# A fused transformer block on one core: two weight slices loaded later, fewer warm-up matmuls, a clamp on another engine

## The chip, the core and the metric

The kernel runs on one core of one Trainium2 chip. The metric is the device time of one execution in microseconds (us); lower is better. The core has five engines that run their own instruction streams and wait for each other through semaphores: TensorE (PE in the profile; PEld is its weight load), VectorE (DVE), ScalarE (ACT), GpSimd (POOL) and SyncE (SP), which here only issues DMA transfers.

## The reference

Everything is bfloat16 outside of the accumulators. With S = 2048 tokens and width 448:

```python
phi = lambda t: jnp.where(t > 0, t + 1, jnp.exp(t)) + 1e-6
q, k, v = split(layernorm(x) @ wqkv)            # 16 heads of 28
pq, pk = phi(q), phi(k)
kv = einsum("bhsd,bhse->bhde", pk, v);  z = einsum("bhsd->bhd", pk)
num = einsum("bhqd,bhde->bhqe", pq, kv)
den = einsum("bhqd,bhd->bhq", pq, z)[..., None] + 1e-6
h = x + (num / den).reshape(B, S, D) @ wo
y = layernorm(h)
h2 = h + (gelu(y @ w_gate) * (y @ w_up)) @ w_down   # inner width 1792
```

So it is a linear attention, whose state `kv` and `z` sums over all tokens, followed by a gated MLP, each behind a layer norm and with a residual.

## The kernel before, in words

The 2048 tokens are 16 tiles of 128. Each piece of work is a named task, and the name says what it is and for which tile. `_Graph` derives the dependencies from the buffers that a task reads and writes, and `ORDERS` gives, engine by engine, the order in which the tasks are issued: five strings, written out in full, for TensorE, ScalarE, VectorE, GpSimd and SyncE. Nothing is decided at run time: an engine takes its tasks in that order and waits at each one for its semaphores. A task that waits therefore holds back everything behind it on its engine. Line numbers below are those of the kernel before. Most matmuls are issued by one helper, so they carry line 430 in the profile; the tile names tell them apart.

**Head.** SyncE and ScalarE issue the loads of x and of the K, V and Q weights. TensorE has nothing to work on yet and runs matmuls on a tile of ones, `warm1` (16, half of the rows each) and `warm0` (`WARM`, line 253, each 128 columns, line 454). For every tile of x VectorE makes the statistics (`bnst`, `bnag`, lines 462 and 463), ScalarE the reciprocal deviation (`ln`, `rstd`), and VectorE (tiles 0 to 3) or GpSimd (the others) the normalised tile (`norm`, lines 486 and 487). Tiles 0 to 3 are transposed on TensorE (`tr0` to `tr3`, line 495) and copied out by ScalarE (`ev`, line 523); the others go through transposing DMAs (`xT`, line 526) after ScalarE has written a copy of their last columns (`dup`, line 525).

**K, V and state.** For each tile `k` and `v` are the matmuls of K and V. Both use the two halves of TensorE's rows at once: in `k` the upper half works on the bank of K and the lower half on that of V, in `v` the other way round. A pass whose bank was last written by the other half waits until that work has drained. For phi(K), ScalarE takes the exponential (`ek`, line 565), GpSimd clamps it (`cl`, line 566), VectorE takes the maximum with K and adds (`ph`, line 568). ScalarE copies V out (`evv`, line 570). `acc..a` and `acc..b` add the tile to the state in two banks. The Q chunks (512 tokens, two passes `qa` and `qb`) are spread among the tiles; the first ones go through `eq` (ScalarE), `cq` (GpSimd, line 626) and `pq` (VectorE, line 627), the later ones through `eq` and `rq` (ScalarE, lines 616 and 617), `cq` and `pq` (VectorE, lines 618 and 619). When all 16 tiles are in, `kz1` and `kz2` (VectorE, lines 642 and 643) write the state with masks.

**Attention output.** For tiles 0 and 1, one at a time: `nd` (TensorE, line 672), `rd` and `om` (VectorE: reciprocal, product, lines 654 and 655), `tro` (transpose on TensorE, line 681), `evo` (ScalarE), `wo` (lines 688 and 689), `hr` (VectorE: residual, line 660), statistics, `normh`, `wrap` (a copy of 64 columns, line 695), `trh` (transpose on TensorE, line 702), `evh` (ScalarE line 707, VectorE line 709). The other tiles go in pairs: `nd..a`, `nd..b`, `rd`, `om`, a transposing DMA for each (`oT`, line 729), `wo..a`, `wo..b`, `hr`, statistics, `normh` on GpSimd, and a transposing DMA (`hT`, line 750).

**MLP.** Token chunks of 2, 2, 4, 4 and 4 tiles. For each chunk `gu` tasks multiply with the gate slice on the upper half of the rows and the up slice on the lower half, `ge` (ScalarE, line 830) is the gelu, `hm` (VectorE, line 832) the product with up, which frees the banks. Two pairs of banks alternate, so a `gu` waits for the `ge` and `hm` of the one two before it. Then come `down` and `out` (residual, line 756) and the store. A table load on ScalarE (`tbl2`, line 850) stands between the exponentials and the first gelu.

**SyncE's queue around the change.** After the twelve `xT`, SyncE issues the loads of `wo` (`dwo` and three more), then seven gate/up slices, a gate half `dwg` and an up half `dwu` for each, 224 KB apiece, then `oT2`, `oT3`, then the whole of `w_down` (`dwd`, 1568 KB), then the later transposes and the stores. Slice k is needed by the k-th pair of matmuls of a `gu` accumulation, so slices 5 and 6 come last in it.

Of the kernel before, what the change touches and what calls it, by code (L numbers as in the profile page):

```python
# [7 lines left out]
ALU = mybir.AluOpType  # L8
# [222 lines left out]
def bass_sequential_preLN__linear_attn_block__glu_gated_geglu__prompt_kernel(  # L231
    nc, A_x, A_wqkv, A_wo, B_x, B_w_gate, B_w_up, B_w_down, out, cfg=None
):
    cfg = dict(cfg or {})
# [678 lines left out]
```

## Time and profile before

| What | Value |
|---|---|
| Three runs, us | 196.69, 196.73, 196.25; median 196.69 |
| The profiled execution, us | 196.70 |
| Its span (first to last instruction), us | 194.9 |
| TensorE busy | 190.3 us, 98% of the span |
| VectorE busy | 116.3 us, 60% |
| ScalarE busy | 78.2 us, 40% |
| GpSimd busy | 42.0 us, 22% |
| Granted TensorE clock, mean over the span | 0.999 |
| Moved by DMA | 17.53 MB, mean 90 GB/s |

How to read it: a row of the timeline gives the start in us from the span's start, the duration, the engine, the line, the operation, output and inputs, the shape, and in brackets the idle time before it and what ended that. A matmul's duration in a row includes its way through the array, so successive ones overlap; the distance between starts is the cost in a sequence. The chain of waits is followed back from the last instruction; a step in it is work that nothing else could have hidden. The span leaves out 1.8 us of the execution's time.

### The profile page before, as it was taken

The numbers are of one execution on the slowest core, as the hardware profiler recorded it, in microseconds if no ns is written. First come the engines' busy times: TensorE is split into PE (matmuls) and PEld (weight loads), VectorE is DVE, ScalarE is ACT, GpSimd is POOL, SyncE is SP. The second block draws the span as 40 slices with busy tenths as digits, with TensorE's granted clock in tenths as the row PEclk, the third lists the DMA queues.
The fourth block names the chain that finished last, engine by engine and source line by source line (L and its number), as shares of the span: only waits on it lengthen the run. The fifth ranks groups of instructions, "written<-read, shape, count | busy, mean of one in ns | idle before, by whom it ended". The sixth has DMA issues, their size and how long they took to land.

```text
span 194.9 us, 5336 instructions
## 1 busy us (share of the span) xinstructions
PE 190.3 (98%) x2192; PEld 137.9 (71%) x2192; DVE 116.3 (60%) x301; ACT 78.2 (40%) x205; POOL 42.0 (22%) x90
## 2 busy tenths in 40 slices
PE   7999999999999999999999999999999999999994
PEld 7556658754588977976675577877778779899554
DVE  2989735368998946843967745756735443431512
ACT  3689866669784212220442441233232442411100
POOL 3099974300050310500500500500500000000000
PEclk9999999999999999999999999999999999999999
DMA  6944558999836052152062250172040000010111
GB/s 191 377 116 97 81 110 185 247 248 205 260 103 110 15 101 50 50 105 62 10 129 46 46 106 2 30 117 51 5 94 28 23 0 0 3 47 3 47 47 47
DMA packets 37256, 17.53 MB, mean 90 GB/s; under 512 B 28272, under 2 KB 36336, under 8 KB 37232
## 3 DMA queue, kind: packets, MB, share of 16 engines
q1 hardware_dynamic: 36352, 16.45, 36.8%
q10 hardware_dynamic: 880, 0.75, 1.2%
q8 instruction: 17, 0.28, 0.6%
q14 instruction: 7, 0.06, 0.1%
HBM read 8.72 MB, written 1.84 MB: 54 GB/s over the span
## 4 chain that ended last, share of the span: by engine, by line
PE 96%; issue 1%; ACT 1%; DVE 1%; POOL 0%; DVEq 0%; ACTq 0%; POOLq 0%
PE ps L430 87%; PE ps L780 6%; PE ps L454 2%; DVE x_sb L660 1%; PE ps L495 1%; ACT xn L617 1%; PE ps L681 0%; ACT xnT L523 0%; PE ps L672 0%; DVE x_sb L756 0%; POOL ones_bf L395 0%; POOL eps_t L398 0%; ACT pqT L616 0%; DVEq L196 0%; ACTq L196 0%
## 5 line engine op out<-in xcount | busy, mean ns | idle before, releaser
L430 PE MATMUL ps<-hnT,wgu_sb 64*128 64x512 bf16 (+1 forms) x980 | 90.4, 333 | 0.0
L430 PEld LDWEIGHTS ps<-hnT,wgu_sb 64*128 64x128 bf16 x980 | 64.5, 94 | 18.6 <-DVE hh L832 1.7
L830 ACT ACTIVATE gl<-ps 128x256 bf16<-128x256 f32 x112 | 36.9, 381 | 89.3 <-PE ps L430 88.2
L832 DVE TENSOR_TENSOR hh<-ps,gl 128x256 bf16<-128x256 f32 x112 | 42.5, 415 | 35.7 <-ACT gl L830 31.5
L430 PE MATMUL ps<-wd_sb,hh 64*128 64x448 bf16 x336 | 34.4, 349 | 0.0
L430 PEld LDWEIGHTS ps<-wd_sb,hh 64*128 64x128 bf16 x336 | 25.6, 94 | 6.2 <-DVE x_sb L756 0.2
L430 PE MATMUL ps<-wkv_sb,xnT 64*128 64x448 bf16 x192 | 22.4, 350 | 0.4 <-ACT xnT L523 0.4
L462 DVE BATCH_NORM_STATS2 st<-x_sb 128x6 f32<-128x448 bf16 x32 | 18.7, 611 | 2.6 <-DMA x_sb<-in_A_x_dram 2.6
L756 DVE TENSOR_TENSOR x_sb<-ps,x_sb 128x448 bf16<-128x448 f32 (+1 forms) x17 | 9.9, 591 | 16.6 <-PE ps L430 9.8
L474 POOL TENSOR_SCALAR ln<-mv 128x2 f32<-128x2 f32 x7 | 1.6, 223 | 75.0 <-DVE mv L463 74.9
L568 DVE SCALAR_TENSOR_TENSOR pk<-ps,tm 128x448 bf16<-128x448 f32 x16 | 9.8, 620 | 9.6 <-POOL tm L566 7.1
L430 PE MATMUL ps<-xnT,wq_sb 64*128 64x512 bf16 x112 | 14.9, 377 | 0.2 <-ACT xn L617 0.2
L430 PEld LDWEIGHTS ps<-wkv_sb,xnT 64*128 64x128 bf16 x192 | 10.1, 94 | 6.3 <-issue 0.8
L430 PE MATMUL ps<-wo_sb,oT 64*128 64x448 bf16 x98 | 12.1, 350 | 0.1
L660 DVE TENSOR_TENSOR x_sb<-ps,x_sb 128x448 bf16<-128x448 f32 x16 | 9.4, 618 | 4.6 <-PE ps L430 4.4
L780 PE MATMUL ps<-wd_sb,hh 128*128 128x448 bf16 (+1 forms) x70 | 10.8, 315 | 0.0
L566 POOL TENSOR_SCALAR tm<-e 128x448 bf16<-128x448 bf16 x16 | 8.9, 559 | 6.4 <-ACT e L565 5.5
L487 POOL TENSOR_SCALAR hn<-x_sb,nm,rs 128x448 bf16<-128x448 bf16 x14 | 10.0, 720 | 0.8 <-POOL rs L476 0.2
L565 ACT ACTIVATE e<-ps 128x448 bf16<-128x448 f32 x16 | 8.5, 541 | 3.5 <-PE ps L430 2.2
L780 PEld LDWEIGHTS ps<-wd_sb,hh 128*128 128x128 bf16 x70 | 6.7, 98 | 4.3 <-issue 0.4
L655 DVE TENSOR_TENSOR o_sb<-ps,rd 128x448 bf16<-128x448 f32 x16 | 9.4, 612 | 0.1
L570 ACT ACTIVATE v<-ps 128x448 bf16<-128x448 f32 x16 | 8.4, 542 | 2.1 <-PE ps L430 2.1
(69 smaller groups left out, 140.4 us busy)
## 6 DMA issues: line engine op xcount, KB each, us to landing
out_dram<-x_sb SPq DMA_DIRECT2D x15, 112.0 KB, 1.7
wgu_sb<-in_B_w_gate_dram SPq DMA_DIRECT2D x7, 224.0 KB, 6.1
wgu_sb<-in_B_w_up_dram SPq DMA_DIRECT2D x7, 224.0 KB, 6.4
wd_sb<-in_B_w_down_dram SPq DMA_DIRECT2D x1, 1568.0 KB, 8.3
x_sb<-in_A_x_dram SPq DMA_DIRECT2D x2, 448.0 KB, 5.3
wkv_sb<-in_A_wqkv_dram ACTq DMA_DIRECT2D x2, 336.0 KB, 3.7
x_sb<-in_A_x_dram SPq DMA_DIRECT2D x3, 224.0 KB, 4.2
wo_sb<-in_A_wo_dram SPq DMA_DIRECT2D x2, 336.0 KB, 4.4
```

The lines of the kernel that those rows point to most:

```text
L430: ins = e.matmul(o_, l_, r_, start=s_, stop=p_, **kw)
L462: op("dve", lambda e: e.bn_stats(st[:, t, :], src_ap), [b_src], [b_st[t]], "%sbnst%d" % ("" if mv is mv1 else "h", t), 0.53, key, after=after)
L487: return lambda e: e.tensor_scalar(dst, src[:, t, :], nm[:, t:t + 1], rs[:, t:t + 1], ALU.add, ALU.mult)
L565: act_exp(lambda e: e.activation(e1[:, ie, :], oK, AF.Exp), bank(bk), [b_e1[ie]], "ek%d" % t, _c_act(D), kk)
L566: op("pool", lambda e: e.tensor_scalar(tm1[:, ie, :], e1[:, ie, :], 1.0 + EPS, 0.0, ALU.min, ALU.max), [b_e1[ie]], [b_tm1[ie]], "cl%d" % t ...
L568: op("dve", lambda e: e.scalar_tensor_tensor(pk[:, i, :, 0:GW], psK3, EPS, tm1[:, ie, :].rearrange("p (g e) -> p g e", g=NG), ALU.max, ALU ...
L655: op("dve", lambda e: e.tensor_tensor(o_sb[:, so, oc:oc + D].rearrange("p (a e) -> p a e", e=28), nd3[:, :, 0:28], rd[:, i, :].unsqueeze(2 ...
L660: op("dve", lambda e: e.tensor_tensor(h_sb[:, u, :], ps[:, b, 0:D], x_sb[:, u, :], ALU.add), bank(b) + [b_x[u]], [b_h[u]], "hr%d" % u, 0.5 ...
L756: op("dve", lambda e: e.tensor_tensor(x_sb[:, t, c0:c1], ps[:, bk, c0:c1], h_sb[:, t, c0:c1], ALU.add), bank(bk) + [b_h[t]], [bo], "out%d% ...
L780: ins = e.matmul(ps[:, bk, c0:c1], hh[:, j, hsl(t)], wd_sb[:, j, c0:c1], start=(j == 0), stop=(j == NJ - 1))
L830: G.add("act", lambda e, gi=gi, cs_=cs_, psG=psG: e.activation(gl[:, gi, cs_], psG[:, cs_], AF.Gelu_apprx_tanh), r=bank(BK_G[i]), w=[b_glh ...
L832: op("dve", lambda e, dst=dst, srcU=srcU, srcL=srcL: e.tensor_tensor(dst, srcU, srcL, ALU.mult), bank(BK_U[i]) + [b_glh], [b_ar[j_][t % HR ...
```

## The change

Five things change together.

1. `WARM` goes from 38 to 33: five fewer matmuls in `warm0`.
2. SyncE issues gate/up slices 0 to 4 as before, then `oT2` and `oT3`, then slices 5 and 6, then `dwd`.
3. The clamps `cl14` and `cl15` are issued on VectorE and no longer on GpSimd.
4. `trh` waits for `wrap` only ahead of its last transpose, the one that reads the wrapped columns.
5. All five order strings are written anew.

What moves in the orders, as far as the prediction speaks of it: on TensorE `acc3a` moves ahead of `k6`, `acc4a` ahead of `k7`, `acc8b` and `acc9b` ahead of `k12` and `v11`; `acc13a` and `acc14a` move ahead of `qa20`, `acc14b` and `acc15b` ahead of `qb20`; `qb31` moves from between `wo2a` and `wo2b` to behind `trh0`; `wo14a`, `wo14b` and the later `down` passes are placed differently among the `gu` tasks. On ScalarE `ek15` moves ahead of `evv15`, `evh0` ahead of `eq14`, and `rq14` behind the gelus of the third `gu`. On VectorE the memset of `pk`'s padding (`pkones`) moves to the head; `pq8` moves up between `om1` and `rd2`; `om4` and `om5` both come before the first `hm`; `cq14` and `cq10` come behind it. On GpSimd some norms and clamps swap places, `negm12` moves ahead of `cq1`, and `powwarm` moves to the head.

```diff
-    WARM = 38
+    GU_AHEAD = 5
+    CL_DVE = cfg.get("cl_dve", (14, 15))
+    WARM = 33
...
-        for k in range(7):
-            prev = [dma(wgu_sb[0:64, k, :], wg3[:, k, :], [b_wg[k]], "dwg%d" % k, 64 * FF * 2, after=prev, key=20.0)]
-            prev = [dma(wgu_sb[64:128, k, :], wu3[:, k, :], [b_wu[k]], "dwu%d" % k, 64 * FF * 2, after=prev, key=20.0)]
+        def load_gu(ks, prev, key):
+            for k in ks:
+                prev = [dma(wgu_sb[0:64, k, :], wg3[:, k, :], [b_wg[k]], "dwg%d" % k, 64 * FF * 2, after=prev, key=key)]
+                prev = [dma(wgu_sb[64:128, k, :], wu3[:, k, :], [b_wu[k]], "dwu%d" % k, 64 * FF * 2, after=prev, key=key)]
+            return prev
+
+        prev = load_gu(range(GU_AHEAD), prev, 20.0)
...
-            op("pool", lambda e: e.tensor_scalar(tm1[:, ie, :], e1[:, ie, :], 1.0 + EPS, 0.0, ALU.min, ALU.max),
+            op("dve" if t in CL_DVE else "pool", lambda e: e.tensor_scalar(tm1[:, ie, :], e1[:, ie, :], 1.0 + EPS, 0.0, ALU.min, ALU.max),
...
-            def ftrh(e):
+            def ftrh(e, W):
                 ins = None
-                for k in (0, 1, 2, 4, 5, 6, 3):
+                for n, k in enumerate((0, 1, 2, 4, 5, 6, 3)):
+                    if n in (0, 6):
+                        W(n)
...
-            G.add("pe", ftrh, r=[b_hn[sh], b_hnd[sh], b_ident], w=bank(bh), name="trh%d" % t, dur=_c_mm(128, 7), key=ka)
+            G.add("pe", ftrh, r=[b_hn[sh], (b_hnd[sh], 6), b_ident], w=bank(bh), name="trh%d" % t, dur=_c_mm(128, 7), key=ka, mw=True, pdt=_c_mm(128))
...
                 if u == 3:
-                    dma(wd_sb[:, :, :], B_w_down.rearrange("(j p) n -> p j n", p=128), [b_wd], "dwd", FF * D * 2, key=ka, after=o_ts)
+                    late = load_gu(range(GU_AHEAD, 7), o_ts, ka)
+                    dma(wd_sb[:, :, :], B_w_down.rearrange("(j p) n -> p j n", p=128), [b_wd], "dwd", FF * D * 2, key=ka, after=late)
```

The order strings in the stretches that the prediction works through, TensorE and ScalarE:

```diff
- v5 k6 qa01 v6 qb01 k7 acc3a acc4a v7 acc4b acc5b k8
+ v5 acc3a k6 qa01 v6 qb01 acc4a k7 acc4b acc5b v7 k8
...
- acc12b acc13b qa20 acc13a acc14a qb20 acc14b acc15b acc15a qa11 nd0 nd1 qb11
+ acc12b acc13b acc13a acc14a qa20 acc14b acc15b qb20 acc15a qa11 nd0 nd1 qb11
...
- qa31 wo2a qb31 wo2b trh1 trh0 nd4a nd4b gu1 gu0 gu3 gu2 gu5 wo4a wo4b
+ qa31 wo2a wo2b trh1 trh0 qb31 nd4a nd4b gu1 gu0 gu3 gu2 gu5 wo4a wo4b
...
- ek14 evv14 evv15 ek15 eq8 rq8 eq6 rq6 evo0 eq12 evo1 eq10 rq10 rq12 hln1 hrstd1 hln0 hrstd0 eq14 evh0 tbl2 ge1_0 ge1_1 rq14
+ ek14 evv14 ek15 evv15 eq8 rq8 eq6 rq6 evo0 eq12 evo1 eq10 rq10 rq12 hln1 hrstd1 hln0 hrstd0 evh0 eq14 tbl2 ge1_0 ge1_1 ge0_1 ge0_0 ge3_1 ge3_0 rq14
```

More of the change, by code (lines that the diff above doesn't have):

```diff
@@ L15 @@
     "warm1 warm0 tr0 tr1 k0 v0 k1 tr2 tr3 v1 k2 acc0a k3 v2 v3 qa00 acc0b acc1b qb00 k4 acc1a acc2a v4 k5 acc2b acc3b"
[4 rows of a table removed]
[4 rows of a table added]
     " wo6b down0b nd8a gu11 nd8b gu10 gu13 gu12 down2a wo8a down2b wo8b gu15 nd10a gu14 nd10b gu17 gu16 gu19 gu18 gu21"
     " wo10a wo10b gu20 nd12a gu23 nd12b gu22 gu25 gu24 gu27 gu26 wo12a down4a wo12b gu29 nd14a gu28 nd14b gu31 down4b"
[36 rows of a table removed]
[31 rows of a table added]
+    "ones eps mhalf mones powwarm ident mask_a opad mask_b mask_c negm4 cl0 norm4 norm5 negm6 cl1 norm6 norm7 negm8"
[4 rows of a table added]
     "dx0 dx1 dx2 dwv_t dx4 dx6 dx8 dx12 dwq dwq_t dwq_u pqones xT4 xT5 xT6 xT7 xT8 xT9 xT10 xT11 xT12 xT13 xT14 xT15"
[3 rows of a table removed]
[3 rows of a table added]
 )
@@ L565, in kv_tile @@
             act_exp(lambda e: e.activation(e1[:, ie, :], oK, AF.Exp), bank(bk), [b_e1[ie]], "ek%d" % t, _c_act(D), kk)
-            op("pool", lambda e: e.tensor_scalar(tm1[:, ie, :], e1[:, ie, :], 1.0 + EPS, 0.0, ALU.min, ALU.max),
-               [b_e1[ie]], [b_tm1[ie]], "cl%d" % t, 0.53, kk)
+            op("dve" if t in CL_DVE else "pool", lambda e: e.tensor_scalar(tm1[:, ie, :], e1[:, ie, :], 1.0 + EPS, 0.0, ALU.min, ALU.max),
+               [b_e1[ie]], [b_tm1[ie]], "cl%d" % t, _c_dve(D, 4.0) if t in CL_DVE else 0.53, kk)
             op("dve", lambda e: e.scalar_tensor_tensor(pk[:, i, :, 0:GW], psK3, EPS, tm1[:, ie, :].rearrange("p (g e) -> p g e", g=NG), ALU.max, ALU.add),
```

83 rows, old and new, of the table ORDERS are left out of this document.

## The prediction

> **What bounds the kernel now.** I read the page first: the span, the busy shares, then the chain of waits.
>
> ```profile
> span 194.9 us, 5336 instructions
> PE 190.3 (98%) x2192; PEld 137.9 (71%) x2192; DVE 116.3 (60%) x301; ACT 78.2 (40%) x205; POOL 42.0 (22%) x90
> ```
>
> TensorE is busy for 98% of the span, and the change removes only five warm-up matmuls from it. So whatever moves must come from the few places where TensorE runs something useless or waits. The chain in order of time (start, duration, what) names them:
>
> ```profile
> 2.00 4.17 PE ps L454 x38
> ...
> 6.68 0.60 ACT xnT L523
> ...
> 7.43 0.95 PE ps L430 x8
> ...
> 48.05 1.03 ACT xn L617
> ...
> 49.21 3.02 PE ps L430 x28
> ...
> 53.91 8.88 PE ps L430 x156
> ```
>
> The first is the head: warm-ups, the transposes tr0 and tr1, their evacuation on ScalarE, and k0 at 7.43. The next is the stretch from 48 to 54, where TensorE hangs on ScalarE (rq10 at 48.05) and VectorE (hr2 and hr3, L660, which free nd4a's banks). From 53.91 on the chain is TensorE alone, save a last residual add; there the swaps of gu, down and wo tasks cost nothing, as gu work covers them, and if that cover is gone a swap costs what rival three prices.
>
> **Head: 33 warm-ups.** Rows of the timeline, the last three of them from the K stage, and TensorE's transposes as min/median/max in ns:
>
> ```profile
> 5.21 0.37 DVE L486 TENSOR_SCALAR xn<-x_sb,mv,rs 128x448 bf16<-128x448 bf16 x1
> 5.66 0.20 ACT L469 ACTIVATE rs<-ln 128x1 f32<-128x1 f32 x1
> 5.97 0.40 DVE L486 TENSOR_SCALAR xn<-x_sb,mv,rs 128x448 bf16<-128x448 bf16 x1
> 6.10 0.96 PE L495 MATMUL ps<-ident,xn 64*128 64x64 bf16 x20
> 17.39 1.29 DVE L627 SCALAR_TENSOR_TENSOR pqT<-ps,tm 112x512 bf16<-112x512 f32 x2
> 17.91 0.40 POOL L481 TENSOR_SCALAR nm<-mv 128x2 f32<-128x2 f32 x2
> 18.74 0.30 PEld L430 LDWEIGHTS ps<-wkv_sb,xnT 64*128 64x128 bf16 x6 [0.29 <-DVE pqT L627]
> L495 PE MATMUL ps<-ident,xn x40: 189/213/260, 6.1 to 10.3; 64*128 64x64 bf16 x24, 64*64 64x64 bf16 x16
> ```
>
> A warm-up costs 4.17/38 = 0.11 us, so five fewer end 0.55 earlier, and tr0 (6.10) could start at 5.55. Its input, norm0, ends at 5.21 + 0.37 = 5.58; with 0.06 for the semaphore (as from pq0's end, 17.39 + 1.29 = 18.68, to k6 at 18.74) tr0 starts at 5.64, 0.46 earlier. The evacuation and k0 follow by the same steps: 6.68 becomes 6.22, 7.43 becomes 6.97. norm1 ends at 6.37 as before: moving the pk memset ahead gains nothing, because norm1 also needs rstd1 (5.66 + 0.20 = 5.86). So tr1 waits until about 6.43, still ahead of k0. Term: -0.46, at most -0.55, and 0 or a loss if the clock does not follow (rival one).
>
> Does it reach the K stage? There TensorE sits just behind POOL and VectorE: k6 starts right after pq0, which follows cq1 and cq0 on POOL. Today negm10 and negm12 (0.40 for the two) run behind them; the new order puts negm12 ahead of cq1, some 0.2, so this point moves by only about 0.25. acc3a, moved ahead of k6, fills part of the hole, and acc4a is then done before k7; I carry -0.40 past it (between -0.25 and -0.46). The other swaps among norms, statistics and xT transposes change no wait that I find on TensorE: 0.
>
> **End of K: the clamp of tiles 14 and 15 on VectorE.**
>
> ```profile
> 36.64 0.54 ACT L565 ACTIVATE e<-ps 128x448 bf16<-128x448 f32 x1 [0.94 <-PE ps L430]
> 37.08 0.98 ACT L570 ACTIVATE v<-ps 128x448 bf16<-128x448 f32 x2
> 37.27 0.56 POOL L566 TENSOR_SCALAR tm<-e 128x448 bf16<-128x448 bf16 x1 [1.78 <-ACT e L565]
> 37.96 0.62 DVE L568 SCALAR_TENSOR_TENSOR pk<-ps,tm 128x448 bf16<-128x448 f32 x1 [1.71 <-POOL tm L566]
> 40.07 1.02 ACT L616 ACTIVATE pqT<-ps 112x1024 bf16<-112x1024 f32 x1 [1.58 <-PE ps L430]
> 40.62 0.63 DVE L642 TENSOR_TENSOR kvz<-ps,mask 113x448 bf16<-113x448 f32 x1 [0.73 <-PE ps L430]
> 41.24 0.42 DVE L618 TENSOR_SCALAR pqT<-pqT 112x1024 bf16<-112x1024 bf16 x1
> ```
>
> Today a clamp takes 0.56 on POOL and ph14 starts 0.78 after ek14's end (37.18 to 37.96). On VectorE no row shows it: between 0.18 (the 0.42 of cq8 by 448/1024 columns) and 0.40 (norm1, same shape). I take 0.2, as cq8 is the same kind of operation; the hop shrinks to about 0.35. That lets acc14a and acc15b stand ahead of qa20 and qb20. But qa20 also needs the bank that evv15 frees, at 37.08 + 0.98 = 38.06; the new order puts evv15 behind ek15, 0.43 later, which eats the 0.40. So qb20 and eq8 stay near 40.07, while kz1 waits only for the single acc15a behind qb20: 40.62 becomes about 40.15. Behind kz1 and kz2 everything (nd0, qb11, eq6, rq10, wo0) shifts by -0.47. This term is thus -0.07, between +0.10 and -0.20.
>
> **The stretch to gu1.** qb31 moves behind trh0, so wo2a and wo2b now adjoin; the last of trh's transposes alone waits for the wrap.
>
> ```profile
> PEld ps L430 <- PE ps L430: 2.2, 6, 0.5
> 53.04 0.22 PE L430 MATMUL ps<-kvz,pqT 64*128 64x116 bf16 x1
> 53.15 0.92 ACT L707 ACTIVATE hnT<-ps 128x896 bf16<-128x896 bf16 x1 [0.43 <-PE ps L702]
> 53.47 0.82 PE L430 MATMUL ps<-kvz,pqT 49*128 49x116 bf16 x15 [0.21 <-DVE x_sb L660]
> 54.08 1.28 ACT L850 ACT_TABLE_LOAD   x1
> 54.13 4.09 PE L430 MATMUL ps<-hnT,wgu_sb 64*128 64x256 bf16 x72
> 55.64 0.62 DVE L655 TENSOR_TENSOR o_sb<-ps,rd 128x448 bf16<-128x448 f32 x1
> 55.87 0.66 ACT L830 ACTIVATE gl<-ps 128x256 bf16<-128x256 f32 x2 [0.50 <-PE ps L430]
> 56.35 0.75 DVE L832 TENSOR_TENSOR hh<-ps,gl 128x256 bf16<-128x256 f32 x2
> ```
>
> On TensorE the hole in nd4a (53.04 to 53.47) goes, as qb31 fills the time of hr2 and hr3. A pair of passes on swapped halves costs a drain: six such waits total 2.2, so 0.37, of which I take 0.3. Net -0.15, and gu1 could start near 53.4 instead of 54.13. But ScalarE decides what comes of it. Now eq14 runs before evh0, which starts at 53.15; qb31's six matmuls (0.65, at 3.02/28 each) leave the way to it, the drain adds 0.3 and the shift takes 0.47, so evh0 starts near 52.3 and ends near 53.2. Behind it come eq14 (1.02, as eq8) to 54.2 and the table load (1.28) to 55.45, so the first gelu starts there instead of at 55.87, and hm1_1 ends near 56.65 instead of 57.10. gu3 needs that bank: gu1 and gu0 are 28 matmuls of 0.055 each, so gu3 is ready at 53.4 + 3.06 = 56.46 and waits until 56.7, where it now starts near 57.19. om4 and om5 both ahead of hm1_0 (one more 0.62, less cq14's 0.42 moved behind) end near 55.9 and push hm1 by at most 0.1. So the shift behind gu3 is -0.45 to -0.5 whatever TensorE gained: this term is 0, between +0.2 and -0.25.
>
> **Gate/up slices 5 and 6 behind oT2 and oT3.** Issues with their time to landing, then throughput by stretch (the last column is GB/s):
>
> ```profile
> 46.73 1.25 SPq L729 DMA_TRANSPOSE oT<-o_sb  x1
> 48.03 0.58 SPq L364 DMA_DIRECT2D wd_sb<-in_B_w_down_dram  x1
> oT<-o_sb SPq DMA_TRANSPOSE x1, 2.6
> wd_sb<-in_B_w_down_dram SPq DMA_DIRECT2D x1, 1568.0 KB, 8.3
> oT<-o_sb SPq DMA_TRANSPOSE x2, 3.7
> 45.00:46.00 1.00, 1.00 (x11) 0.34 (x8) 1.00 (x4) 1.00 (x2) 0.00 (x0) 1.00 0.99 237
> 50.00:54.50 4.50, 4.23 (x62) 2.66 (x58) 4.27 (x12) 3.35 (x7) 0.00 (x0) 1.00 1.02 335
> 61.77 1.81 PE L430 MATMUL ps<-wo_sb,oT 64*128 64x448 bf16 x14
> ```
>
> The first three rows of landing times are oT3, wd and the pair oT5, oT4. oT3 lands at 46.73 + 2.6 = 49.3, while wo2a stands behind qa31, whose eight matmuls begin at 49.21; both move by the same 0.47, so an earlier landing gains nothing: 0. The cost lies behind. Four loads, each some 0.63 of SyncE (wd's 0.58 and 0.05 between issues), go out from 47.5 on and move 4 x 0.23 MB at 237 GB/s = 3.9 us, so slice 6 lands near 52.5; gu1, from 53.4, reaches slice 5 after ten matmuls, 0.55 later. Some 1.4 us of cover; without it gu1 waits for the lack. wd goes out near 50.0 instead of 48.03, moves 1.6 MB at 335 GB/s = 4.8 us from 52.5 on and lands near 59 with the tail it has now (48.03 + 8.3 = 56.3). oT5 and oT4, issued near 55.2 and 56.5 (today 3.7 to land), stand behind it on the same queue and, taken in order, land near 60; wo4a needs both at 61.3. Taken at 0, bounds 0 and +1.5. [...]
>
> **The sum.** -0.40 (head as carried) - 0.07 (end of K) + 0 + 0 = -0.47. The profiled execution took 196.70, its span 194.9 and 1.8 around it; the median of the three runs, 196.69, is practically that. 196.70 - 0.47 = 196.2. The terms' ends give 196.0 to 196.4 as this case's own range.
>
> **Rivals.** One, the other side: the clock opens later. All 38 warm-ups ran at 0.11, while the transposes fall from 260 to 189 ns, so TensorE seems to speed up only while tr0 and tr1 run, 4.1 to 5.1 us after warm0 began at 2.00; 38 barely sufficed. If 33 fall short, k0 and what follows run at about half speed until such a stretch has passed again: at least 0, at most 5.1 us at half speed, 2.5 lost; the middle, 1.3, gives 196.2 + 1.3 = 197.5. It decides as soon as the opening needs more than the 3.6 us of 33 warm-ups. For it: the late opening. Against: the transposes and k0 follow within half a microsecond. [...]
>
> Two: the head's gain does not pass POOL and VectorE near k6 and evv15. For it: the 0.06 between pq0 and k6. Only acc15a and qb31 are left: 196.6.
>
> Three: wd holds oT5 and oT4 back. If they land at 62.3 instead of 60, wo4a waits 1.0: 197.2. It decides from 61.3 on.
>
> Four: the gelu chain follows TensorE (eq14 does not hold the table load), and the -0.15 at nd4a and the filled wait before gu1 count too: gu1's -0.7 survives, 196.70 - 0.75 = 195.95.
>
> **How the numbers follow.** Main case 0.40, rival one 0.17, two 0.12, three 0.09, four 0.22. A measurement of this kernel tells about 0.3%, 0.6 us, from no change; below 196.1 is faster. Of the main case a third, 0.13, falls below that, with rival four 0.35. Same: 0.27 + 0.12 = 0.39. Slower: 0.17 + 0.09 = 0.26. The range 195.8 to 197.7 holds the main case, two, three, most of four and the lower half of one, leaving out about 0.15.
>
> **What would show it.** Right: tr0 near 5.64 and k0 near 6.97; kz1 near 40.15; no hole inside nd4a; first gelu near 55.45; wd landing near 59 and wo4a without a wait. Wrong: the matmuls of k0 to k1 lasting twice as long (one); k6 still near 18.7 (two); a gap ahead of wo4a or inside gu1 ended by a DMA (three); the gelu at 55.1 or earlier (four).

## The result, and the profile after

| | before | after |
|---|---|---|
| Median of 22 runs each, us | 196.43 (196.15 to 197.15) | 196.86 (196.56 to 198.29) |
| Ratio | | 1.0026, 95% interval 1.0015 to 1.0037 |
| Profiled execution, us | 196.70 | 196.71 |

The kernel became slower by about a quarter of a per cent; 0.24% faster had been forecast. One remark is needed to read the times: executions of one kernel differ by about half a microsecond in when k0, the first matmuls of K, starts; those of before lie mostly near 196.2 or near 196.7 us, and its profiled one starts late, that of after early. So the two profiles end level while the medians do not.

The page of after, span and busy time:

```profile
span 195.0 us, 5326 instructions
PE 190.3 (98%) x2187; PEld 127.6 (65%) x2187; DVE 117.1 (60%) x303; ACT 77.9 (40%) x205; POOL 41.6 (21%) x88
```

Five instructions fewer on TensorE and yet the same busy time: this line doesn't tell where the time of the five warm-ups went. The chain of waits of after does, in order of time (start, duration, what):

```profile
6.46 0.41 PE ps L497 x10
...
6.88 0.95 PE ps L432 x8
...
49.22 4.98 DMA wgu_sb<-in_B_w_up_dram
54.19 0.05 issue
54.24 8.43 PE ps L432 x135
```

k0 starts at 6.88 where it started at 7.43. But between 48 and 54, where the chain of before ran through rq10, `qa31` and nd4a, there is now a transfer: the up half of slice 6, issued at 49.22, lands at 54.19, and `gu1`, which had started at 53.22, waits for it. What TensorE's weight loads of after waited for (us in total, times, longest):

```profile
PEld ps L432 <- DVE hh L842: 5.0, 21, 0.3
...
PEld ps L432 <- DMA oT<-o_sb: 0.3, 1, 0.3
PEld ps L432 <- DMA wgu_sb<-in_B_w_up_dram: 0.3, 1, 0.3
```

The two DMA rows are new. The row for `hh` was, in before:

```profile
PEld ps L430 <- DVE hh L832: 1.7, 9, 0.2
```

(These are waits of the weight loads. TensorE's tasks lose 0.25 to `hm` in what follows, at gu2 and gu5, and 0.17 further on, so most of the 5.0 us don't show as a gap between matmuls.) The first two rows of this stretch of after's timeline tell what a good part of it is about, VectorE's clamps `cq14` and `cq10` and GpSimd's `normh3` and `normh2`:

```profile
56.37 1.81 POOL L489 TENSOR_SCALAR hn<-x_sb,nm,rs 128x448 bf16<-128x448 bf16 x2
56.48 1.12 DVE L625 TENSOR_SCALAR pqT<-pqT 112x1024 bf16<-112x1024 bf16 x2
...
57.52 0.74 DVE L842 TENSOR_TENSOR hh<-ps,gl 128x256 bf16<-128x256 f32 x2
58.18 0.26 DVE L759 COPY hn<-hn 128x448 bf16<-128x448 bf16 x1
58.31 0.11 PEld L432 LDWEIGHTS ps<-hnT,wgu_sb 64*128 64x128 bf16 x4 [0.25 <-DVE hh L842]
```

In before the same two norms take 1.41. Beside them VectorE runs only products that read PSUM, and its next product of the packing work comes after them:

```profile
57.11 1.41 POOL L487 TENSOR_SCALAR hn<-x_sb,nm,rs 128x448 bf16<-128x448 bf16 x2
58.92 0.68 DVE L619 TENSOR_TENSOR pqT<-xn,pqT 112x1024 bf16<-112x1024 bf16 x1
```

The start of TensorE's tasks against before, worked out from the traces, in us (negative is earlier). Four later kernels of this study stand beside it:

| Task | before at | after | e6 | e9 | e12 | e14 |
|---|---|---|---|---|---|---|
| k0 | 7.43 | -0.54 | -0.44 | -0.41 | -0.51 | -0.48 |
| nd0 | 41.44 | -0.72 | -0.39 | -0.37 | -0.47 | -0.43 |
| gu1 | 54.13 | -0.91 | -0.58 | -0.56 | -0.66 | -0.62 |
| gu0 | 55.66 | -0.64 | -0.58 | -0.56 | -0.66 | -0.62 |
| gu5 | 60.25 | -0.49 | -0.50 | -0.48 | -0.38 | -0.53 |
| wo4a | 61.77 | -0.39 | -0.21 | -0.45 | -0.38 | -0.51 |
| gu4 | 63.42 | -0.13 | -0.20 | -0.44 | -0.37 | -0.50 |
| down2a | 84.63 | -0.13 | -0.20 | -0.18 | -0.34 | -0.50 |
| gu54 | 179.96 | -0.06 | -0.13 | -0.08 | -0.32 | -0.50 |
| down12 | 181.65 | +0.04 | -0.04 | +0.02 | -0.32 | -0.50 |

In after 0.91 us had been won by gu1. Slice 6 took 0.27 of it back, gu2 and gu5 0.25 (waits for `hm0_0` and `hm3_0`), wo4a 0.26 (the transpose `oT5`), and what comes behind, wo10 and the last `gu54` above all, 0.17.

### The profile page after: what moved, and what is told of

Same layout as the page of the kernel before. It is cut to its first block, busy times and chain, and to the rows that moved or that the text cites. A ratio compares the mean times of both kernels' runs of the same rounds, so it can differ in the third digit from the quotient of the medians.

```text
span 195.0 us, 5326 instructions
## 1 busy us (share of the span) xinstructions
PE 190.3 (98%) x2187; PEld 127.6 (65%) x2187; DVE 117.1 (60%) x303; ACT 77.9 (40%) x205; POOL 41.6 (21%) x88
## 4 chain that ended last, share of the span: by engine, by line
PE 90%; DMA 4%; DVE 2%; SPq 1%; issue 1%; ACT 0%; DVEq 0%
PE ps L432 83%; PE ps L790 6%; DMA wgu_sb<-in_B_w_up_dram 3%; DMA x_sb<-in_A_x_dram 2%; SPq L366 1%; PE ps L497 1%; DVE o_sb L662 0%; DVE pqT L626 0%; DVE st L464 0%; DVE pqT L625 0%; SPq L738 0%; PE ps L679 0%; DVE rd L661 0%; DVE xn L488 0%; DVE x_sb L766 0%
## 5 line engine op out<-in xcount | busy, mean ns | idle before, releaser
L432 PE MATMUL ps<-hnT,wgu_sb 64*128 64x512 bf16 (+1 forms) x980 | 91.9, 333 | 0.1
L432 PEld LDWEIGHTS ps<-hnT,wgu_sb 64*128 64x128 bf16 x980 | 61.7, 94 | 23.1 <-DVE hh L842 5.0
L432 PE MATMUL ps<-wd_sb,hh 64*128 64x448 bf16 x336 | 35.2, 349 | 0.0
L432 PEld LDWEIGHTS ps<-wd_sb,hh 64*128 64x128 bf16 x336 | 21.1, 94 | 11.2 <-DVE x_sb L766 0.2
L432 PE MATMUL ps<-wo_sb,oT 64*128 64x448 bf16 x98 | 12.9, 350 | 0.2
L483 POOL TENSOR_SCALAR nm<-mv 128x2 f32<-128x2 f32 x13 | 2.9, 226 | 39.5 <-DVE mv L465 39.2
L432 PEld LDWEIGHTS ps<-wo_sb,oT 64*128 64x128 bf16 x98 | 6.1, 94 | 4.3 <-PE ps L432 1.5
```

What stands on the lines that cost most here:

```text
L432: ins = e.matmul(o_, l_, r_, start=s_, stop=p_, **kw)
L483: op("pool", lambda e: e.tensor_scalar(nm[:, a:b], mv[:, a:b, 0], -1.0, None, ALU.mult), b_mv[a:b], b_nm[a:b], "%snegm%d" % ("" if mv is m ...
```

## The experiments

All runs are timed beside the kernel before on the same chip, in five rounds. The labels carry the order in which they were made; here they stand by question. "Shift" is the column of the table above.

### The head

**e4** is the kernel before with `-    WARM = 38` / `+    WARM = 33` alone, **e7** with 20.

> The kernel before with 33 warm-ups, nothing else. Theory W: some executions at 197.2 us and more, median ratio 1.001 to 1.003. Theory T: no execution loses; ratio 0.998 to 1.000, as k0 starts up to 0.45 us earlier.

> The kernel before with 20 warm-ups. Theory W: the time falls into two groups, one near 196.4 us and one 1.2 to 1.7 us above it, and the upper group holds more than the third that 33 warm-ups gave, half or more. Against it: one group only, or an upper group no larger than with 33.

e4: 196.46, ratio 1.0013 (0.9995 to 1.0030). Nine executions lie at 196.16 to 196.72, three at 197.37, 197.75 and 197.96, which is 0.9 to 1.5 above the middle of the nine. None of these three was profiled; that TensorE reached full speed late in them is inferred from e7. For the 197.96 there is another candidate, as its mean granted clock was 0.991 and that of the others 1.00. e7: 198.52, ratio 1.0093 (1.0066 to 1.0121), every execution 1 us or more above before's median. The stretch from 7 to 9 us of before and then of e7 (behind the comma stand PE's busy time and, in brackets, its matmuls; the third number from the end is the granted clock):

```profile
7.00:9.00 2.00, 1.58 (x19) 0.68 (x16) 2.00 (x8) 1.60 (x6) 0.08 (x1) 1.00 1.09 377
```
```profile
7.00:9.00 2.00, 1.94 (x10) 0.56 (x12) 2.00 (x8) 1.59 (x5) 0.01 (x1) 1.00 1.08 369
```

Ten matmuls where nineteen ran, at a granted clock of 1.00 in both: the granted clock doesn't show whether TensorE has reached full speed, the distance between matmuls does. What the prediction and the expectations call the clock's opening shows in this distance alone. So what rival one describes happens (in e7 the shift goes from -0.48 at k0 to +1.66 at k6), and if it is behind e4's three executions, its price with 33 is 0.9 to 1.5, around the 1.3 that it was given.

e7 and e4 also show what the profile of before hid. The warm-ups of before, and those of e14, which has 38 too (duration min/median/max in ns, first and last start):

```profile
L454 PE MATMUL ps<-ones_bf x38: 289/314/315, 1.9 to 5.9; 128*128 128x128 bf16 x38
```
```profile
L456 PE MATMUL ps<-ones_bf x38: 219/246/314, 1.9 to 4.9; 128*128 128x128 bf16 x38
```

In e14's execution TensorE sped up during the warm-ups: from 3.93 on they follow each other at 0.056 us instead of 0.107. All 38 were done a microsecond earlier, and k0 began at 6.95, nearly as early as with 33 in after. Of the eleven profiles with 38 warm-ups five are like this one (e6, e9, e10, e12, e14: the spacing falls at 3.8 to 5.2 us, k0 starts at 6.90 to 7.02), and six like before (the slow spacing to the end or nearly so, k0 at 7.25 to 7.43). So with 38 about half of the executions start k0 about as early as 33 ever does, since norm0 then holds tr0 (in e14 norm0 ends at 5.68 and tr0 starts at 5.74). 33 gains only against the other half, 0.34 at k0 in e4's profile and 0.54 in after's, and, if it is behind e4's three executions, loses 0.9 to 1.5 where full speed comes too late.

**e2** is after with 38.

> The changed kernel with 38 warm-ups again. Theory W: 33 warm-ups let the clock open late in part of the executions; with 38 the executions above 197.2 us go and the ratio to the kernel before falls to about 1.000. Theory T: the head starts 0.45 us later in executions whose clock opens late, but the wait for the slices and for the transposes absorbs it; the ratio stays at 1.002 to 1.003.

196.99, ratio 1.0031 (1.0018 to 1.0044), the highest of seven 197.61: no execution far above the rest, but the loss is still there. In its profile, which is that highest one, gu1 loses 0.73 to slice 6 and wo4a 0.5 to the transpose. The warm-ups aren't what makes the change slower.

### The loads

**e3** is before with only the four loads moved, **e1** is after with all seven slices ahead of `oT2`.

```diff
- dwg4 dwu4 dwg5 dwu5 dwg6 dwu6 oT2 oT3 dwd        (e3; e1 is the reverse, on after)
+ dwg4 dwu4 oT2 oT3 dwg5 dwu5 dwg6 dwu6 dwd
```

> The kernel before with slices 5 and 6 loaded behind oT2 and oT3, nothing else. Theory T: gu1 waits 0.0 to 0.3 us for slice 6, wo4a 0.3 to 0.6 for the transposes behind wd: ratio 1.002 to 1.004. Theory W: 1.000.

> The changed kernel with all seven gate/up slices ahead of oT2 and oT3 again; warm-ups, clamps and orders stay changed. Theory T (transfers): the late slices hold gu1 for 0.3 us and the transposes behind wd hold wo4a for another 0.3, so this kernel gains 0.4 to 0.6 us over the changed one and comes to 0.999 to 1.001 of the kernel before; gu1 and wo4a show no wait for a DMA. Theory W (warm-ups): the transfers are not what costs; it stays at about 1.0026, with single executions above 197.2 us as in the changed kernel.

e3: 197.56, ratio 1.0049 (1.0036 to 1.0062). What its weight loads waited for:

```profile
PEld ps L433 <- DMA wgu_sb<-in_B_w_up_dram: 0.9, 1, 0.9
```

The slice lands 5.68 us after its issue and gu1 stands for 0.8. Taken alone this part costs more than the whole change does. Yet e1, which takes it out of after, is worse: 198.48, ratio 1.0109 (1.0082 to 1.0136). There `oT2` and `oT3` stand behind late slices and land 6.0 and 5.2 us after their issue (2.5 in after), wo2a waits 1.8 for them, and gu1 starts 1.35 later than before. The reason is in SyncE's queue, rows of before and then of after:

```profile
28.64 3.19 SPq L364 DMA_DIRECT2D wo_sb<-in_A_wo_dram  x4
31.87 0.50 SPq L364 DMA_DIRECT2D wgu_sb<-in_B_w_gate_dram  x1
```
```profile
27.89 3.31 SPq L528 DMA_TRANSPOSE xnT<-xn  x2
31.25 2.42 SPq L366 DMA_DIRECT2D wo_sb<-in_A_wo_dram  x4
33.72 0.50 SPq L366 DMA_DIRECT2D wgu_sb<-in_B_w_gate_dram  x1
```

In after the last x transposes are late, because their norms are (`norm12` behind `cl7`, `norm15` behind `cl8` on GpSimd), so every weight load behind them starts 1.9 to 2.6 us later. So two parts of the change belong together: the norms delay the queue, and moving the two slices behind `oT3` repairs that for `oT2` and `oT3`, at the price of a wait for slice 6.

**e8** is before with the new ScalarE, VectorE and GpSimd orders up to the last K tiles, **e5** is after with the orders of before there (both clamps kept on VectorE) and all slices ahead, **e6** is e5 with 38 warm-ups.

> The kernel before with the new orders of ScalarE, VectorE and GpSimd up to the last K tiles, nothing else (clamps on GpSimd, 38 warm-ups, seven slices ahead). Theory N: the wo load is issued 2 to 3 us later, oT2 and oT3 land behind the slices, wo2a waits 0.5 to 1.5 us: ratio 1.003 to 1.008. Theory R: 1.000.

> The changed kernel with the orders of ScalarE, VectorE and GpSimd up to the last K tiles taken from the kernel before (so norm12 and norm15 come early again), and all seven slices ahead of oT2. Theory N: the new order of norms delays the transposes xT12 to xT15 and with them every weight load by 2.6 us, and that is what made the late slices necessary and the loss; here the wo load is issued near 28.3, wo2a, gu1 and wo4a wait for no DMA, and the executions whose clock opens in time come to 195.7 to 196.1 us, 0.996 to 0.998 of the kernel before; about a third lose another 1.3 us to the late clock. Theory R: the new orders of the stretch to gu1 cost time of their own (the gelu and product chain); then it is no better than 1.000 even where the clock opens in time.

> The same with 38 warm-ups. Theory N: no execution with a late clock, all within 0.5 us, ratio 0.997 to 0.999. Theory R: 1.000 or above.

e8: 197.40, ratio 1.0047 (1.0033 to 1.0061); its wo load is issued at 32.02. In its profile, which is its fastest execution, the end stands at +0.49: 0.15 of this is there at nd0, 0.19 comes in wo2a, which waits for `oT3`, and 0.15 at trh1. So these swaps, costed at 0 in the prediction, cost half a microsecond alone in the profile, and 0.9 by the ratio. e5: 196.67, ratio 1.0022 (1.0003 to 1.0041). e6: 196.97, ratio 1.0025 (1.0015 to 1.0035). No load is late in either (wo issued at 28.15 and 28.23, no DMA row among the waits), and still they aren't faster than before: e6 has -0.58 at gu1 and -0.04 at the end. Something behind gu1 takes it.

### Behind gu1

In e6 a weight load of gu5 waited 0.4 for `hm3_0`, and the task lost 0.29. VectorE and GpSimd there:

```profile
57.97 0.29 DVE L761 COPY hn<-hn 128x448 bf16<-128x448 bf16 x1
58.18 1.04 DVE L628 TENSOR_TENSOR pqT<-xn,pqT 112x1024 bf16<-112x1024 bf16 x1
59.14 0.26 DVE L761 COPY hn<-hn 128x448 bf16<-128x448 bf16 x1
59.33 0.74 DVE L844 TENSOR_TENSOR hh<-ps,gl 128x256 bf16<-128x256 f32 x2
```
```profile
56.66 2.02 POOL L491 TENSOR_SCALAR hn<-x_sb,nm,rs 128x448 bf16<-128x448 bf16 x2
```

The product `pq10` takes 1.04 where its like takes 0.68, and the two norms 2.02 where they take 1.41. Which of the two engines pays differs: the first norm, at 56.66, begins 0.02 behind the clamps `cq14` and `cq10`, which take 0.41 and 0.42 as they do alone, and it takes 1.23 itself; the second takes 0.80, and there the product pays. **e9** moves the product back:

```diff
- hm0_0 wrap3 pq10 wrap2 hm3_1 hm3_0 pq12 pq14 hm2_1
+ hm0_0 wrap3 wrap2 hm3_1 hm3_0 pq12 pq14 pq10 hm2_1
```

> The kernel of e6_early_loads_warm38 (norm and transpose order of before, seven slices ahead of the o transposes, 38 warm-ups, everything from the last K tiles on in the order of the change) with one VectorE instruction moved: the pack product pq10 stands behind pq14 again and no longer between wrap3 and wrap2. In the profile of e6 pq10 took 1.04 us (58.18 to 59.22) beside GpSimd's norms, hm3_1 began at 59.33 though its gelu had ended at 58.95, and gu5 waited 0.40 us for hm3_0. Theory V (what is lost behind gu1 in e6 comes from VectorE's order): gu5's excess falls from 0.33 to at most 0.1, the shift of wo4a against before goes from -0.21 to about -0.45 and is carried, and the time falls by 0.2 to 0.25 against e6's 196.97: 196.7 to 196.8, ratio 1.0010 to 1.0015. Theory C (the gelus follow TensorE, so whatever arrives early at gu1 is paid back in this chain): hm3_0 still ends near 60.0, gu5 still waits about 0.3, and the time stays at 196.9 to 197.0, ratio 1.0025.

**e10** is e9 with `out10 hm54_0 out11 hm54_1` in place of `out11 out10 hm54_0 hm54_1`.

> e9 with a second VectorE pair back in the order of before: out10, hm54_0, out11, hm54_1 in place of out11, out10, hm54_0, hm54_1. In e6 the first matmul of the last down tiles waited 0.4 us for the residual sum out10, which ended at 181.36 behind out11, against 180.87 before; the gap between gu54 and down12 grew by 0.09. Theory V: down12's excess in front falls by 0.09 again, and the time is 0.05 to 0.1 below e9's: 196.6 to 196.7, ratio 1.0005 to 1.001; no wait of the change is then left and the kernel stands level with before. Theory C for this place (the PSUM rows of the last down tiles are bound by the gelu of slice 54, not by the sums): no change against e9.

e9: 196.72, ratio 1.0021 (1.0011 to 1.0032); e10: 196.99, ratio 1.0026 (1.0016 to 1.0036). gu5's wait is gone and wo4a stands at -0.45, as theory V said, but the time doesn't follow: 0.26 of it is lost at gu12, to which VectorE's `hm10_1` comes late.

```profile
82.20 0.76 DVE L844 TENSOR_TENSOR hh<-ps,gl 128x256 bf16<-128x256 f32 x2 [0.37 <-ACT gl L842]
...
83.01 0.22 PEld L434 LDWEIGHTS ps<-hnT,wgu_sb 64*128 64x128 bf16 x6 [0.36 <-DVE hh L844]
```

The gelu named as the releaser had ended 0.46 earlier (81.74); what held VectorE isn't settled. It is the same in e10, whose own edit did nothing: gu54 keeps its 0.09.

**e11** is e9 with the orders of before from the third gelu slice on, on all engines. **e12** is before with one piece of the change: `trh1 trh0` ahead of `qb31`, with the split wait and what it needs on ScalarE and VectorE.

```diff
- qa31 wo2a qb31 wo2b trh1 trh0 nd4a                      (e12, TensorE)
+ qa31 wo2a wo2b trh1 trh0 qb31 nd4a
- evh1 cq14 hbnst2 ... om5 hm1_0 hm1_1 om4 hm0_1 hm0_0 wrap3 wrap2 pq12 hm3_1 hm3_0 pq14 pq10   (VectorE)
+ evh1 hbnst2 ... om4 hbnag3 om5 hm1_0 hm1_1 cq14 cq10 hm0_1 hm0_0 wrap3 wrap2 hm3_1 hm3_0 pq12 pq14 pq10
```

> The kernel of e9_product_back with the orders of before from the third gelu slice on: TensorE from gu30, ScalarE from ge5, VectorE from hm2, GpSimd from vpe2, the SP queue from oT5. What is left of the change is the end of K and the stretch to the first slice (with seven slices ahead of the o transposes and 38 warm-ups). In the profile of e9 TensorE stood at -0.41 against before at k0, -0.56 at gu1, -0.44 at gu8, and then gave back 0.26 at gu12 (wait for hm10_1), 0.08 at gu14 to wo10b, 0.03 at gu34 and 0.09 at gu54. The kernel with 33 warm-ups alone carried its -0.25 from gu1 to the end without a loss, so the orders of before pass an early arrival on. Theory V (the loss behind gu1 lies in the new orders): the shift of the end is as large as that of gu8, that is 0.0 to 0.1 better than the shift at k0; the lower of the two groups of times goes from 196.6 to 196.1, median 196.1 to 196.5, ratio 0.999 to 1.000. Theory C (VectorE and ScalarE cannot pass on an arrival this early in whatever order): gu12 or gu5 waits 0.2 to 0.3 again, the end is 0.3 to 0.45 behind the shift of k0, and the time stays at 196.6 to 197.0, ratio 1.002.

> The kernel before with one piece of the change alone: the transposes trh1 and trh0 ahead of the projection qb31, with the early start of the first six transposes, and what this needs on ScalarE and VectorE up to the third gelu slice (evh0 ahead of eq14, rq14 behind ge3_0, om4 and om5 ahead of hm1_0, cq14 and cq10 behind hm1_1, the pack products behind hm3_0). Orders of the head, of the K tiles and of everything behind the third slice, the loads and 38 warm-ups are those of before. In e9 this stretch brought TensorE from -0.37 at nd0 to -0.56 at gu1, and the end of K cost 0.04 (-0.41 at k0). Theory V: the gap in front of nd4a falls from 0.68 to about 0.24, gu1 stands 0.15 to 0.2 better than k0, gu3 gives 0.08 back, and the end is 0.1 to 0.15 better than the shift at k0: lower group near 196.0, median 196.0 to 196.4, ratio 0.9985 to 0.9995, the one part of the change that pays. Theory C: the gelu chain begins no earlier, since its table load stands behind eq14, and the 0.15 are given back at gu2, gu5 and gu12: ratio 1.000 to 1.001.

e11: 196.77, ratio 1.0011 (1.0002 to 1.0020). From gu8 to the end it loses 0.02, as theory V said. But it comes to gu8 0.18 later than before, so it doesn't test whether the orders of before pass an early arrival on (e14 does), and 0.19 goes at gu2, a wait of the size that theory C expected at gu5 or gu12. e12: 196.56, ratio 1.0008 (0.9999 to 1.0017), with the same loss at gu2. VectorE and GpSimd of e12 there:

```profile
56.57 1.15 DVE L620 TENSOR_SCALAR pqT<-pqT 112x1024 bf16<-112x1024 bf16 x2
57.64 0.73 DVE L836 TENSOR_TENSOR hh<-ps,gl 128x256 bf16<-128x256 f32 x2
```
```profile
56.48 1.82 POOL L489 TENSOR_SCALAR hn<-x_sb,nm,rs 128x448 bf16<-128x448 bf16 x2
```

Two clamps that take 0.42 each alone need 1.15 together (they overlap by 0.08), and the norms 1.82. That it isn't the place of the clamps alone, e6 shows: there they stand ahead of hm0 too, take 0.75 together, and gu2 loses nothing. **e13** moves the clamps behind the products they hold up (`hm3_1 hm3_0 cq14 cq10 pq12 hm2_0 hm2_1 pq14 pq10`, `rq14` behind `ge2_0`), **e14** moves `pq14 pq10` further, behind `hm6_0`.

> The kernel of e12_transposes_first_alone with VectorE's clamps cq14 and cq10 moved from behind hm1_1 to behind hm3_0, pq14 and pq10 behind hm2_1, and ScalarE's rq14 behind ge2_0. In the profile of e12 cq10 took 0.78 us (56.93 to 57.72) while GpSimd ran the norm of tile 3 (56.48 to 57.44, 0.96 us against 0.71 elsewhere); hm0_1 began at 57.64 though its gelu had ended at 57.12, and gu2 waited 0.23 for it; the end stood at -0.32 where k0 had -0.51. Theory P (the clamp and GpSimd's norm hold each other up, and this is the loss behind gu1): normh3 takes 0.71, hm0_1 begins within 0.2 of its gelu's end, gu2 waits at most 0.05, and the end of the profile stands 0.0 to 0.1 better than k0 against before; the lower group of times falls from 196.37 to 196.1 to 196.2, median 196.1 to 196.4, ratio 0.9990 to 1.0000. Theory C (the gelus of the second and third slice follow TensorE and set hm0 and hm3 in any order): gu2 or gu5 still waits about 0.2 and the ratio stays at 1.0008.

> The kernel of e13_clamps_behind with the pack products pq14 and pq10 moved once more, from behind hm2_1 to behind hm6_0, where VectorE has nothing to do for 3.3 us. In the profile of e13 the wait at gu2 was gone (normh3 0.713 us, hm0_1 0.10 behind its gelu), but pq14 and pq10 (62.00 to 63.29) then stood ahead of hm5_1 and of the residual sums hr5 and hr4, and nd6a waited 0.35 for hr4, which ended at 65.02 against 64.78 before. Theory P (only the packing work put between the products of the first slices and the norms costs time there): no wait above 0.1 remains behind gu3, the end of the profile stands 0.0 to 0.15 better against before than k0 does; the lower group of times is at 196.05 to 196.2, ratio 0.9985 to 1.0000. Theory D (what arrives early at gu1 is taken by the next place in the chain each time): a wait of 0.2 or more appears at another place behind gu5, and the ratio is 1.0005 to 1.0015.

GpSimd and VectorE of e13, and what gu4's successor nd6a waited for:

```profile
56.83 1.41 POOL L489 TENSOR_SCALAR hn<-x_sb,nm,rs 128x448 bf16<-128x448 bf16 x2
```
```profile
62.00 1.29 DVE L621 TENSOR_TENSOR pqT<-xn,pqT 112x1024 bf16<-112x1024 bf16 x2
63.21 0.75 DVE L836 TENSOR_TENSOR hh<-ps,gl 128x256 bf16<-128x256 f32 x2
63.87 1.15 DVE L662 TENSOR_TENSOR x_sb<-ps,x_sb 128x448 bf16<-128x448 f32 x2
```
```profile
65.07 0.22 PEld L432 LDWEIGHTS ps<-kvz,pqT 64*128 64x128 bf16 x8 [0.43 <-DVE x_sb L662]
```

With nothing of VectorE's SBUF work beside them the norms are back at 1.41 and the wait at gu2 is gone; e13 loses 0.33 further on because the products now stand ahead of `hr5` and `hr4`. Its time, 196.83, ratio 1.0023 (0.9999 to 1.0046), contains one execution of 198.98, whose mean granted clock was 0.991 while the others have 1.00; why, no run shows. e14: **196.42, ratio 0.9993 (0.9985 to 1.0002)**. Its weight loads wait for `hh` as little as those of before:

```profile
PEld ps L432 <- DVE hh L836: 1.9, 10, 0.2
```

From gu5 to the end it loses 0.03 (last column of the table), and theory P holds: the packing work was all that the first slices lost. What this piece of the change is worth is small, -0.02 at the end against k0: it wins 0.19 between nd0 and gu1, gu3 gives back 0.08 to the gelu chain, the K stage had lost 0.05 and the rest goes in steps of 0.01 to 0.02. And e14 carries its early arrival, -0.53 at gu5, to the end through the orders of before, where e9, with the new orders and -0.44, lost 0.26 at gu12: the losses behind the first slices belong to the new orders. e14 is level with before and, by the two ratios, 0.3% faster than the changed kernel; no version was found that is clearly faster than before.

**e15** does the same in the changed kernel, 33 warm-ups and late slices included.

> The changed kernel itself (33 warm-ups, five slices ahead of the o transposes, its orders) with the same positions of the packing work: cq14 and cq10 behind hm3_0, pq14 and pq10 behind hm6_1, rq14 behind ge2_0. In its profile gu2 waited 0.15 and gu5 0.10 behind cq10 (0.78 us beside the norm of tile 3) and pq10, then wo4a 0.26 for the o transpose of tile 5, which landed at 61.68 behind the load of the down weights. Theory P with the queue as second limit: the two waits go, wo4a begins 0.25 earlier and waits 0.45 to 0.5 for the same transpose, and the time stays at 196.8 to 196.9, ratio 1.002 to 1.003. Rival (the packing work is the limit, the transpose follows it): the transpose is issued and lands 0.2 to 0.3 earlier too, wo4a waits no longer than now, and the time falls to 196.6, ratio 1.001.

197.29, ratio 1.0050 (1.0029 to 1.0071), against both theories. Its chain of waits has

```profile
49.29 5.63 DMA wgu_sb<-in_B_w_up_dram
```

so gu1 stands 0.93, and from there on it is as late as before (+0.09 at gu0, no wait at gu2 or wo4a, +0.19 at gu54). The landing of slice 6 took 4.98, 5.44, 5.63 and 5.68 us in the four profiles that have it late (after, e2, e15, e3); after's is the shortest. So e15 doesn't decide between its theories: with slices that late, neither of the waits could show. That its median is 0.4 us above that of after stays open; the intervals of the two ratios overlap, and no instruction ahead of gu1 differs.

## Why the prediction was wrong

**Head, "Term: -0.46".** In the profiled execution it came out (tr0 at 5.67, forecast 5.64; k0 at 6.88, forecast 6.97; tr1, at 6.46 near the forecast, ended at 6.87, just ahead of k0). As a difference of the two kernels it failed: the term was measured on one execution, in which 38 warm-ups ran at 0.107 us to the end. Kernels with the same head and 38 warm-ups (e12, e14) have k0 nearly as early, so the faster executions of before, none of which was profiled, most likely have it too; and e4 gains nothing in the median (196.46 against 196.53 for before beside it). The row of the profile that could have warned is the one quoted there: all 38 at 0.11 us, at the slow spacing; nothing said that this was so in every execution. Rival one was rightly priced; executions about a microsecond or more above the rest, none of them profiled, are 1 of 22 in after, 3 of 12 in e4, 2 of 12 in e5 and 2 of 9 in e15. With the same 38 the last warm-up starts anywhere from 4.9 to 5.9, so TensorE speeds up at different times from run to run; what sets the time no run shows.

**"The other swaps among norms, statistics and xT transposes change no wait that I find on TensorE: 0."** This step failed. In e8 the swaps cost 0.15 by nd0, and they delay the x transposes, which SyncE's queue passes on to the loads of wo and of the slices (28.64 to 31.25 in after). e8 as a whole: +0.49 in its profile, 0.9 by the ratio.

**"slice 6 lands near 52.5 ... Some 1.4 us of cover."** This step failed too. It landed at 54.19. The throughput was near the assumed 237 GB/s; in after, the stretch from the first of the four issues to the landing:

```profile
47.30:54.20 6.90, 6.53 (x76) 3.44 (x75) 6.44 (x19) 5.12 (x10) 0.00 (x0) 1.00 0.85 219
```

6.90 us at 219 GB/s are 1.51 MB, of which the four loads are 0.92. What the rest is, the sizes of the packets in the trace tell: 0.43 MB are rows of wd (896 bytes each), issued 0.64 behind slice 6, and 0.13 MB pieces of `oT3` (256 bytes each). The first row of the four loads moved only at 48.68, 1.4 after its issue, and the last ended at 53.71; wd's rows had been moving since 51.95, and 484 of its 1792 were through when slice 6 landed. The step let the transfers pass one after the other, but the last piece of an early load moves beside a good part of a later one. Whether rows of wd overtook rows of slice 6 on one and the same DMA engine the trace doesn't tell.

**"taken in order, land near 60; wo4a needs both at 61.3."** wd landed at 59.05 (forecast 59, by luck: it moved from 51.95 to 58.68 and not in 4.8 us from 52.5 on), but oT5 at 61.68, 5.6 us after its issue, and wo4a waited 0.26. The order in which they pass was the author's assumption, and no run shows it for a single DMA engine: in after pieces of 256 bytes, the size of `oT5`'s and `oT4`'s, move from 56.86 on, ahead of the next transposes' issue at 58.47, while rows of wd move until 58.68. Rival three named the right wait at a quarter of its price.

**The stretch to gu1** was right in its mechanism: the hole in nd4a is gone, and kz1 starts at 40.04 (forecast 40.15; a clamp takes 0.28 on VectorE, estimated at 0.2). That the table load holds the first gelu shows in e14, where the gelu follows it at 55.45. In after the load ended at 55.14, and that the gelu's 55.32 is near the forecast 55.45 is luck: it waited for gu1, which stood for slice 6. **"the shift behind gu3 is -0.45 to -0.5 whatever TensorE gained"** was the value at gu5 (-0.49) by luck as well: gu2 still stood at -0.64, and the waits for hm0 and hm3 took it to -0.39 at wo4a. In e14, without these waits, it is -0.54 at gu2 and -0.50 to the end. What failed is the sentence ahead of it: that om4 and om5 "push hm1 by at most 0.1" was true of hm1, and the step stopped there. cq14 and cq10 stand ahead of hm0, and beside GpSimd's norm cq10 takes 0.78 instead of 0.42; pq10 stands ahead of hm3, at its usual 0.68 in after and at 1.04 in e6. In before none of this packing work ran beside the norms. Shown by e12 to e14.

**"there the swaps of gu, down and wo tasks cost nothing"**: what comes behind wo4a cost 0.17 in after, and e9 lost 0.26 at gu12. e14, with the orders of before, loses 0.03 from gu5 on.

So against a head term that isn't there in the median stand, in the profiled execution, 0.27 at gu1 (0.73 to 0.93 in three other profiles with late slices), 0.25 at gu2 and gu5, 0.26 at wo4a and 0.17 further on. The range of the main case, 196.0 to 196.4, doesn't follow from its terms either: their bounds add up to 195.8 at one end and, with the loads' +1.5, to 198.2 at the other.

Not run alone was the clamp of tiles 14 and 15 on VectorE. e11 has it, with the new end of K and a few moved passes of the state, and e12 lacks all of these; both lose 0.04 to 0.05 between k0 and nd0, and their ratios are 1.0011 and 1.0008. So with the old order of the norms this piece shows no worth. In after nd0 stands 0.18 better than k0 (forecast 0.07); which part of the change does that stays open.

## What to carry to other kernels

A term read off a single execution is a difference of kernels only if the kernel before is in the same condition in every run: look at where its runs group before crediting the head. Cost a moved instruction by what is queued behind it on its engine and on the queue that its result releases, and look at what GpSimd runs at the same time: the same clamp was 0.42 us in one place and 0.78 in the next. And check an early arrival against the next three consumers, since here each wait that was removed uncovered another until e14 cleared the whole stretch.

## What was unexpected of the hardware

- VectorE and GpSimd slow each other: a 112x1024 clamp took 0.42 us alone and up to 0.78 beside a GpSimd norm, a 112x1024 product 0.68 and 1.04, the norm 0.71 and 0.80 to 1.23. Either side can pay: clamps that began just ahead of the norm kept their 0.42. VectorE's products `hm`, which read PSUM, don't change (0.42; none of the 112 in after takes over 0.43). Why the two engines slow each other no run shows.
- When TensorE reaches full speed isn't in the granted clock (1.00 in before and in e7), only in the spacing of the matmuls (0.107 against 0.056 for 128 columns), and with the same 38 warm-ups it came at 3.8 us in e6 and not by 5.85 in before.
- Two transposes of 128x512 behind a 1568 KB load took 5.0 and 5.6 us to land in after, 5.5 and 6.0 in e2, 4.6 and 3.9 in e15; the two ahead of it took 2.5.
